# A mixer block with MLP on one core: first weight split over two DMA rings, and a new work order

## The chip, the core and the metric

The kernel runs on one core of one Trainium2 chip. The core has a matrix engine (PE, with weight loads shown as PEld), a vector engine (DVE), an activation engine (ACT), a general engine (POOL) and a sync engine (SP). Transfers between device memory and on-chip memory are issued by SP or by ACT; each of the two has a DMA queue ("ring") of its own. The metric is the device time of one execution, in microseconds (us): the median over several runs.

## The reference

`x` is 2048 tokens of 512 features, in bf16. The computation:

```python
h  = gelu(layernorm(x) @ w1)                       # w1: 512 x 512
# four quarters of h's features are shifted along the tokens by +1, -1, +2, -2
hs = concat(shift(h0, 1), shift(h1, -1), shift(h2, 2), shift(h3, -2)) @ w2   # w2: 512 x 512
x1 = x + hs
out = x1 + gelu(layernorm(x1) @ w3) @ w4           # w3: 512 x 1792, w4: 1792 x 512
```

The layer norms have no weights. The statistics are over the 512 features of a token.

## The kernel before

**Tiles.** The tokens form 16 tiles of 128 (t = 0 to 15). A tile passes through nine stages:

- Its load `dma_x` brings it into `x_sb`.
- Layer norm 1 (`ln`, lines 384 to 465). The statistics come from DVE (`bn_stats`, L416, and `bn_aggr`, L418) or from ACT (two activations with an accumulator, L395 and L400, and then small DVE operations, L408 and L412). POOL raises the variance to the power -1/2 (L423), and DVE, ACT or POOL normalizes (L445, L454, L457).
- A transpose puts features on the partitions, in `xnT`. It is done either by PE with an identity matrix (`pe_transpose`, L490, followed by a copy out of PSUM on DVE or ACT, L498), or by a DMA transpose issued on SP (L463).
- `up1` (`mm_up`, L626) multiplies by `w1`, and ACT applies gelu (L641) into `hT`.
- `mix` (`mm_mix`, L666) multiplies shifted slices of `hT` by `w2`; DVE adds `x` (L673 or L677) and makes `x1`. `mix` of tile t needs `hT` of tiles t-1, t and t+1.
- Layer norm 2 and its transpose work in the same way. Its numbers q run from 16 to 31: q = 16 + t.
- `up2` (L626) multiplies by `w3`, and ACT applies gelu (L641) into `h2T`.
- `down` (`mm_down`, L695) multiplies by `w4`, and DVE adds `x1` (L703).
- A DMA stores the tile.

Neighbouring tiles are grouped for `up1` and `up2` (`GROUPS`), in ones, twos and fours. In the written order `up1:6` means group 6 of layer 1. PSUM holds three double banks (`y_ps`) for transposes and `up`, and two banks (`o_ps`) for `mix` and `down`. So a `mix` waits until DVE has added up the `mix` or `down` two before it.

**The first tile** is special. It is centred only (L431), in two halves, and transposed in two halves (`sa:0`, `sb:0`). It is multiplied by `w1` in two halves, `ra:0` and `rb:0` (L528). The first half, two matmuls, reads the first half of `w1`; the second half reads the other. The scale goes into the gelu (L569), and `th:0` (L594) transposes the result.

**The order of PE** is written out in `SCRIPT`, from left to right. It begins with matmuls on zeros (`warm:9`, L720), which keep PE occupied until the first tile is ready; `ty:n` is a PE transpose of layer-norm output n, in a double bank. Output numbers that are not in `SCRIPT` as `sa` or `ty` are transposed by DMA.

**The order of the other engines** is not written out. `Program.order` gives each operation a due time, worked back from the PE order; `Program.place` then plays the program forward with its own estimates of durations and landings, and lets each engine take the most urgent operation that is ready. Engines run their lists in order, and wait with semaphores. `BIAS` adds to the due time of single operations. `NORM`, `EVAC`, `STAT_ACT`, `NMR` and `HEV` say which engine does which small operation, by q.

**The order of the loads** is `LOADS`, from left to right for each issuing engine. `@act` puts a load on ACT's ring; all others are on SP's. A suffix `a` or `b` means the first or second half of a weight's rows, and `x4-5` is one transfer of two tiles. An entry `tpN` fixes the place of a DMA transpose among the loads; if N is transposed by PE, the entry has no effect. Loads are issued ahead of all else on their engine (`op.first`). SP's list is in order: a DMA transpose that waits for its tile holds up every load behind it.

```python
LOADS = """
x1 x2 tp2 x0@act w1a w1b x3 x4-5 tp5 w2a w2b x6-7 w3 tp17 w4a x8-10 w4b tp6 x11-12 tp1 tp16 x13-15
"""
```

In this list `tp6` is the only `tp` entry that has an effect: the others are PE transposes.

Of the kernel before, what the change touches and what calls it, by code (L numbers as in the profile page):

```python
# [14 lines left out]
class Op:  # L15


    def __init__(self, name, eng, fn, reads, writes, dur, queue):
        self.name, self.eng, self.fn = name, eng, fn
        self.reads, self.writes = list(reads), list(writes)  # L20
        self.dur, self.queue = dur, queue
        self.idx = 0
        self.prio = 1e9
        self.first = None

class Program:
# [2 lines left out]

    HOP = {"pe": 200.0, "dve": 155.0, "act": 220.0, "pool": 120.0, "sp": 70.0}  # L30
    LOOK = {"dve": 300.0, "act": 300.0}
    DUE = 164483.0
    BEGIN = {"sp": 30.0, "act": 150.0, "pe": 400.0, "dve": 150.0, "pool": 450.0}
    ENTRY = 1900.0
    COLD, RESTART = 4300.0, 800.0
    LAG = {"load": 750, "tp": 700}

    def __init__(self):
        self.ops = []
# [12 lines left out]
    def order(self):  # L52
# [58 lines left out]
        assert seen == len(self.ops), "cycle"  # L111
        if self.DUE:

# [37 lines left out]
    def place(self, succs, order_only):  # L151

        npend = [len(d) for d in self.preds]
        ready = [0.0] * len(self.ops)
        cands = {e: [] for e in ENGINES}
        for op in self.ops:
            if npend[op.idx] == 0:
                cands[op.eng].append(op)
        free = dict(self.BEGIN)
        rings = {"sp": [], "act": []}  # L160
        fed = {}
        clock = moved = last = self.total = 0.0
        out = []

        def finish(limit):
            nonlocal clock
            while True:
                heads = {e: r[0] for e, r in rings.items() if r}
                if not heads:
                    return None  # L170
                live = [e for e in heads if heads[e][0] <= clock]
                later = min([h[0] for h in heads.values() if h[0] > clock], default=1e18)
                if not live:
                    if later > limit:
                        return None
                    clock = later
                    continue
                first = min(live, key=lambda e: heads[e][1])
                step = heads[first][1] * len(live)
                ends = clock + step <= min(later, limit)  # L180
                if not ends:
                    step = min(later, limit) - clock
                for e in live:
                    heads[e][1] -= step / len(live)
                clock += step
                if ends:
                    return rings[first].pop(0)[2]
                if clock >= limit:
                    return None

        def release(op, o, at):
            npend[o.idx] -= 1
            if at is not None:
                ready[o.idx] = max(ready[o.idx], at)
            if npend[o.idx] == 0:
                cands[o.eng].append(o)

        def land(op):
            nonlocal moved, last
            if op.queue == "tp":  # L200
                at = max(clock + 500.0, op.start + 2450.0, last + 600.0) + self.LAG["tp"]
            elif op.name.startswith("out"):
                at = clock + 300.0
                self.total = max(self.total, at)
            else:
                moved += op.dur
                at = clock + 600.0 + min(600.0, 0.3 * moved) + (600.0 if op.dur > 1400.0 else 0.0)
                at += self.LAG["load"] if moved > 1200.0 else 50.0
            if op.queue != "tp":
                last = max(last, at)  # L210
            op.landed = at
            for j in succs[op.idx]:
                if (op.idx, j) not in order_only:
                    release(op, self.ops[j], at + 30.0)

        while len(out) < len(self.ops):
            while True:
                best = None
                for e in ENGINES:
                    if cands[e]:  # L220
                        t = max(free[e], min(ready[o.idx] for o in cands[e]))
                        if best is None or t < best[0]:
                            best = (t, e)
                op = finish(best[0] if best else 1e17)
                if op is None:
                    break
                land(op)
            t, e = best
            look = self.LOOK.get(e, 1.0)
            op = min((o for o in cands[e] if ready[o.idx] <= t + look), key=lambda o: (o.prio, o.idx))  # L230
            cands[e].remove(op)
            start = max(free[e], ready[op.idx])
            op.start = start
            out.append(op)
            if op.queue:
# [6 lines left out]
                rings[e].append([start + (1400.0 if tp else 1000.0), work, op])  # L242
# [12 lines left out]
        while (op := finish(1e17)) is not None:  # L255
            land(op)
        self.seq = out
        return out

GROUPS = {1: (1, 1, 1, 1, 2, 1, 4, 2, 2, 1), 2: (2, 4, 4, 2, 4)}  # L260
NORM = {0: "act", 3: "act", 7: "pool", 8: "act", 9: "pool", 10: "pool", 11: "pool", 12: "pool", 14: "act", 15: "act", 16: "pool", 18: "act", 19: "act", 24: "pool", 25: "act", 26: "pool", 27: "pool", 29: "pool", 30: "pool", 31: "act"}
EVAC = {0: "both", 1: "both", 2: "both", 4: "both", 8: "both", 9: "dve", 10: "dve", 11: "dve", 12: "dve", 13: "dve", 14: "dve", 16: "dve", 17: "dve", 19: "both", 20: "both", 21: "both", 22: "both", 23: "both", 24: "dve", 25: "both", 27: "both", 29: "both", 30: "both", 31: "both"}
STAT_ACT = (0, 7, 9, 12, 13, 15, 18, 21, 25, 29, 30)
TAIL = (256, 160, 96)
NMR = {0: "pool", 1: "pool", 3: "pool", 5: "pool", 6: "pool", 7: "pool", 8: "pool", 9: "pool", 11: "pool", 13: "pool", 14: "pool", 15: "pool", 16: "pool", 17: "pool", 18: "pool", 20: "pool", 21: "pool", 22: "pool", 26: "pool", 27: "pool", 28: "pool", 29: "pool", 31: "pool"}
# [12 lines left out]
down:12-15  # L278
"""

def bass_standalone__mixer_s_mlp__prompt_kernel(nc, x, w1, w2, w3, w4, out):
# [14 lines left out]
    with ExitStack() as es:  # L296
        sb = lambda name, shape, dt: es.enter_context(nc.sbuf_tensor(name, shape, dt))
# [22 lines left out]
        warm = sb("warm", [P, 1], F32)  # L320
# [410 lines left out]
        for step in SCRIPT.split():  # L731
            kind, n = step.split(":")
# [139 lines left out]
```

## Time and profile before

| what | value |
|---|---|
| median of 4 runs | 135.58 us (135.18 to 135.88) |
| the profiled execution: its time | 135.58 us |
| the profiled execution: its span, first to last instruction | 134.3 us |
| PE busy, share of span | 131.1 us, 98% |
| DVE busy | 50.6 us, 38% |
| ACT busy | 58.6 us, 44% |
| POOL busy | 29.9 us, 22% |
| bytes moved by DMA | 12.19 MB |

The span leaves out 1.28 us of the execution's time. The profile page gives the busy time of each engine, the chain of work that ended last (followed back from the last instruction), and groups of instructions by code line with their count, busy time and mean duration. Other answers of the trace give the instructions in order of time, and the busy time and DMA rate in a stretch of the span. A row of the time-ordered list has the start, the length, the engine, the line, the operation and its tiles, the count, and in brackets the idle time before it and what ended that.

### The profile page before, as it was taken

The page shows a single profiled execution, that of the slowest core. Times are in us where ns is not written, and L with a number is a line of the kernel's source. Part 1 is how long each engine was busy: PE and PEld are TensorE (multiplying, and loading weights), DVE is VectorE, ACT ScalarE, POOL GpSimd, SP SyncE. Part 2 cuts the span into 40 slices and gives each one's busy share as a digit, 9 for nine tenths or more (in the row PEclk, how much of TensorE's full clock was granted, in tenths as well). Part 3 has the DMA queues.
Part 4 walks back from the last instruction along what each step waited for, and adds up shares of the span by engine and source line. Part 5 has one row for each costly group of instructions (what it writes and reads, how often), then busy time and mean ns, then how long its engine had stood idle before and what let it go on. Part 6 is the DMA issues. An engine that isn't in the chain of part 4 may idle for free.

```text
span 134.3 us, 2001 instructions
## 1 busy us (share of the span) xinstructions
PE 131.1 (98%) x776; PEld 71.7 (53%) x789; DVE 50.6 (38%) x134; ACT 58.6 (44%) x92; POOL 29.9 (22%) x68
## 2 busy tenths in 40 slices
PE   8999999999999999999999999999999999999994
PEld 3387687544666444478444444444444444444464
DVE  2799995765188930070061004232222200012223
ACT  6788359998535275547315554000000155520000
POOL 2444469983003850005010002100000000000000
PEclk9999999999999999999999999999999999999999
DMA  5899998445542134100311000311111100001112
GB/s 156 286 388 397 353 298 244 78 95 102 103 94 81 38 77 83 39 0 9 74 39 39 0 0 0 77 41 44 39 39 63 54 0 0 0 5 39 39 39 78
DMA packets 21289, 12.19 MB, mean 91 GB/s; under 512 B 13856, under 2 KB 20768, under 8 KB 21280
## 3 DMA queue, kind: packets, MB, share of 16 engines
q1 hardware_dynamic: 20704, 11.80, 32.1%
q10 hardware_dynamic: 576, 0.26, 0.7%
q8 instruction: 6, 0.10, 0.3%
q14 instruction: 3, 0.02, 0.1%
HBM read 6.82 MB, written 2.10 MB: 66 GB/s over the span
## 4 chain that ended last, share of the span: by engine, by line
PE 94%; DMA 3%; issue 1%; SPq 1%; DVE 0%
PE y_ps L626 46%; PE o_ps L695 36%; PE o_ps L666 10%; DMA w_sb<-in_w_dram 3%; PE y_ps L490 1%; PE y_ps L528 1%; SPq L368 1%; DVE o_sb L703 0%; PE o_ps L594 0%; SPq L857 0%
## 5 line engine op out<-in xcount | busy, mean ns | idle before, releaser
L626 PE MATMUL y_ps<-xnT,w_sb 128*128 128x512 bf16 (+2 forms) x421 | 63.4, 308 | 0.2
L626 PEld LDWEIGHTS y_ps<-xnT,w_sb 128*128 128x128 bf16 x424 | 38.3, 98 | 24.8
L641 ACT ACTIVATE h2T<-y_ps 128x1024 bf16<-128x1024 f32 (+1 forms) x29 | 28.6, 994 | 48.8 <-PE y_ps L626 48.6
L695 PE MATMUL o_ps<-w_sb,h2T 128*128 128x512 bf16 (+3 forms) x247 | 48.6, 355 | 0.3
L695 PEld LDWEIGHTS o_ps<-w_sb,h2T 128*128 128x128 bf16 x252 | 23.5, 98 | 24.7
L703 DVE TENSOR_TENSOR o_sb<-o_ps,x_sb 128x512 bf16<-128x512 f32 (+3 forms) x18 | 11.4, 632 | 47.5 <-PE o_ps L695 47.5
L423 POOL TENSOR_TENSOR rstd<-mv,neghalf 128x1 f32<-128x1 f32 x21 | 11.5, 551 | 22.9 <-DVE mv L418 13.2
L666 PE MATMUL o_ps<-w_sb,hT 128*128 128x512 bf16 x59 | 14.9, 379 | 0.3
L416 DVE BATCH_NORM_STATS2 st<-x_sb 128x6 f32<-128x512 bf16 x21 | 14.0, 677 | 2.7 <-DMA x_sb<-in_x_dram 2.6
L423 POOL TENSOR_TENSOR rstd<-vpe,neghalf 128x1 f32<-128x1 f32 x11 | 6.0, 550 | 29.6 <-DVE vpe L412 29.5
L673 DVE SCALAR_TENSOR_TENSOR x_sb<-o_ps,x_sb 128x512 bf16<-128x512 f32 x5 | 3.4, 686 | 19.2 <-PE o_ps L666 19.2
L641 ACT ACTIVATE hT<-y_ps 128x512 bf16<-128x512 f32 (+1 forms) x10 | 8.1, 808 | 5.7 <-PE y_ps L626 5.6
L677 DVE TENSOR_TENSOR x_sb<-o_ps,x_sb 128x512 bf16<-128x512 f32 x11 | 7.6, 687 | 4.8 <-PE o_ps L666 4.7
L666 PEld LDWEIGHTS o_ps<-w_sb,hT 128*128 128x128 bf16 x64 | 6.0, 98 | 5.7
L457 POOL TENSOR_SCALAR xn_buf<-x_sb,rstd,nmr 128x512 bf16<-128x512 bf16 x11 | 8.4, 770 | 0.8 <-DVE nmr L450 0.4
L400 ACT ACTIVATE junk<-x_sb 128x512 bf16<-128x512 bf16 x11 | 6.9, 626 | 2.3 <-DVE x_sb L673 2.2
L454 ACT ACTIVATE xn_buf<-x_sb,nmr,rstd 128x512 bf16<-128x512 bf16 x8 | 6.3, 806 | 0.3 <-POOL nmr L450 0.2
L445 DVE TENSOR_SCALAR xn_buf<-x_sb,mv,rstd 128x512 bf16<-128x512 bf16 x12 | 5.3, 443 | 2.8 <-POOL rstd L423 2.5
L720 PE MATMUL o_ps<-zeros 128*128 128x512 bf16 x9 | 4.0, 631 | 0.4 <-DVE zeros L347 0.4
L395 ACT ACTIVATE junk<-x_sb 128x512 bf16<-128x512 bf16 x6 | 3.7, 624 | 0.7 <-DMA x_sb<-in_x_dram 0.7
L418 DVE BATCH_NORM_AGGREGATE mv<-st 128x2 f32<-128x9 f32 x21 | 3.8, 188 | 0.3
L450 POOL TENSOR_SCALAR nmr<-mv,rstd 128x1 f32<-128x1 f32 x13 | 3.4, 266 | 0.7
(34 smaller groups left out, 28.8 us busy)
## 6 DMA issues: line engine op xcount, KB each, us to landing
out_dram<-o_sb SPq DMA_DIRECT2D x15, 128.0 KB, 1.7
w_sb<-in_w_dram SPq DMA_DIRECT2D x1, 1792.0 KB, 9.6
w_sb<-in_w_dram SPq DMA_DIRECT2D x2, 896.0 KB, 11.5
w_sb<-in_w_dram SPq DMA_DIRECT2D x4, 256.0 KB, 4.9
x_sb<-in_x_dram SPq DMA_DIRECT2D x3, 256.0 KB, 4.8
x_sb<-in_x_dram SPq DMA_DIRECT2D x2, 384.0 KB, 8.5
x_sb<-in_x_dram SPq DMA_DIRECT2D x3, 128.0 KB, 2.6
xnT<-xn_buf SPq DMA_TRANSPOSE x24, 2.5
```

The lines of the kernel that those rows point to most:

```text
L400: (lambda d: (lambda e: e.activation(d, src, ACT_F.Square, accum_out=sums[:, q, 1:2])))(junk[:, b, :]),
L416: pg.add("dve", f"bnst{q}", lambda e: e.bn_stats(st9[:, q, 0:6], src), reads=rs, writes=[(("st", q), 0)], dur=605)
L423: lambda e: e.tensor_tensor(col(rstd), var, neghalf[:], ALU.pow),
L445: lambda e: e.tensor_scalar(dst, src, mv[:, q, 0:1], rstd[:, q : q + 1], ALU.subtract, ALU.mult),
L454: f = lambda e: e.activation(dst, src, ACT_F.Identity, bias=nmr[:, q : q + 1], scale=rstd[:, q : q + 1])
L457: f = lambda e: e.tensor_scalar(dst, src, rstd[:, q : q + 1], nmr[:, q : q + 1], ALU.mult, ALU.add)
L626: ins = e.matmul(y_ps[:, p, W * i : W * (i + 1)], wsb[:, dc, P * fc : P * (fc + 1)], src[:, dc, P * t0 : P * t0 + W], start=(dc == 0), sto ...
L641: (lambda d, s: (lambda e: e.activation(d, s, ACT_F.Gelu_apprx_tanh)))(dst, ysrc),
L666: ins = e.matmul(dst, hT[:, j, c0 : c0 + P], w2_sb[:, j, :], start=(j == 0), stop=(j == DC - 1))
L677: f = lambda e: e.tensor_tensor(x1_sb[:, t, :], dst, x_sb[:, t, :], ALU.add)
L695: ins = e.matmul(dst, h2T[:, fc, P * t : P * (t + 1)], w4_sb[:, fc, cs], start=(fc == 0), stop=(fc == FC - 1))
L703: (lambda d, c: (lambda e: e.tensor_tensor(o_sb[:, oi, c], d, x1_sb[:, t, c], ALU.add)))(dst, cs),
```

## The change

- **Loads.** `w1`'s first half goes on ACT's ring, behind `x0` and ahead of `x3`, which moves there too. SP's ring has `x1`, `x2`, `w1`'s second half, and then single tiles and halves in another order. `w4`'s second half stands ahead of `w3`, which is loaded in two halves. There are 19 loads on SP and 3 on ACT, where there were 15 and 1. Of the `tp` entries only `tp16` has an effect (the others are PE transposes).
- **PE's order.** 11 matmuls on zeros in place of 9. PE transposes are 0 to 7 and 17, where they were 0 to 5, 16 and 17; so outputs 6 and 7 leave the DMA transposes and output 16 joins them. The groups of layer 1 keep their counts (six ones, three twos, one four) but stand in another order; those of layer 2 too (two twos, three fours). `mix`, `up` and `down` are in another order.
- **The small operations** are dealt to the engines anew, by tables.
- **The planner** that orders DVE, ACT, POOL and SP has other constants: a limit on the descriptors outstanding on SP's ring, another estimate of landings, another `DUE`, and biases on single operations. None of these is executed on the chip; they alter the order of each engine's list.

```diff
-    DUE = 164483.0
+    DUE = 67895.5
...
-    LAG = {"load": 750, "tp": 700}
+    RING = 150.0
+    LAG = {"load": 750, "tp": 350}
...
             if op.queue == "tp":
-                at = max(clock + 500.0, op.start + 2450.0, last + 600.0) + self.LAG["tp"]
+                turned = max(clock + 500.0, op.start + 2450.0, last + 500.0, turned + 480.0)
+                at = turned + self.LAG["tp"]
...
-                at += self.LAG["load"] if moved > 1200.0 else 50.0
+                at += 50.0 if moved <= 1200.0 else self.LAG["load"] - 300.0 if moved <= 4000.0 else self.LAG["load"] if moved <= 11000.0 else self.LAG["load"] + 650.0
...
+            if e == "sp":
+                over = op.descs - self.RING + sum(h[2].descs * h[1] / h[3] for h in rings[e])
+                at = clock
+                for h in rings[e]:
+                    if over <= 0:
+                        break
+                    at = max(at, h[0])
+                    n = h[2].descs * h[1] / h[3]
+                    at += h[1] * min(1.0, over / n)
+                    over -= n
+                    if over <= 0:
+                        start = max(start, at)
...
-GROUPS = {1: (1, 1, 1, 1, 2, 1, 4, 2, 2, 1), 2: (2, 4, 4, 2, 4)}
-NORM = {0: "act", 3: "act", 7: "pool", 8: "act", 9: "pool", 10: "pool", 11: "pool", 12: "pool", 14: "act", 15: "act", 16: "pool", 18: "act", 19: "act", 24: "pool", 25: "act", 26: "pool", 27: "pool", 29: "pool", 30: "pool", 31: "act"}
-EVAC = {0: "both", 1: "both", 2: "both", 4: "both", 8: "both", 9: "dve", 10: "dve", 11: "dve", 12: "dve", 13: "dve", 14: "dve", 16: "dve", 17: "dve", 19: "both", 20: "both", 21: "both", 22: "both", 23: "both", 24: "dve", 25: "both", 27: "both", 29: "both", 30: "both", 31: "both"}
-STAT_ACT = (0, 7, 9, 12, 13, 15, 18, 21, 25, 29, 30)
+GROUPS = {1: (1, 1, 1, 1, 1, 1, 2, 2, 4, 2), 2: (2, 4, 2, 4, 4)}
+NORM = {0: "act", 4: "act", 7: "pool", 9: "act", 11: "act", 13: "pool", 15: "act", 18: "pool", 19: "pool", 20: "pool", 21: "pool", 22: "pool", 24: "pool", 25: "pool", 27: "pool", 28: "act", 29: "act", 30: "act"}
+EVAC = {0: "dve", 2: "dve", 3: "dve", 5: "both", 7: "dve", 8: "both", 9: "both", 10: "dve", 11: "dve", 12: "both", 13: "both", 16: "both", 18: "both", 20: "dve", 21: "dve", 22: "both", 25: "dve", 26: "both", 27: "both", 28: "both", 31: "dve"}
+STAT_ACT = (0, 5, 6, 9, 11, 14, 15, 18, 22, 23, 25, 27, 28, 30, 31)
...
-HEV = {0: "dve", 4: "dve"}
-BIAS = {}
+HEV = {0: "dve", 1: "dve", 3: "dve", 5: "dve", 6: "dve"}
+BIAS = {"mean6": -214.811, "msq0": -704.156, "msq1": -1177, "msq3": -700, "msq8": 436, "nmr3": 872, "nmr5": -1644.96, "norm13": 252.578, "norm2": 835.299, "sum15": 16, "tp23": 764, "tp5": 433, "vpe11": -1349, "vpe2": 59, "x1_12": -296.043, "x1_2": 193, "x1_3": -58}
 LOADS = """
-x1 x2 tp2 x0@act w1a w1b x3 x4-5 tp5 w2a w2b x6-7 w3 tp17 w4a x8-10 w4b tp6 x11-12 tp1 tp16 x13-15
+x0@act tp0 x1 x2 w1b x6 x4 w2b tp6 w2a x5 tp2 x7 w4b tp2 x8 w3a w3b x9 x13 tp16 x11-12 w4a w1a@act tp7
+x14-15 x10 tp2 x3@act
 """
 SCRIPT = """
-warm:9 sa:0 sb:0 ty:1 ra:0 rb:0 ty:2 up1:1 th:0 up1:2 mix:0 ty:3 ty:5 mix:1 ty:4 up1:3-4 ty:16 mix:2 ty:17
-mix:3 up2:0 mix:4 up1:5 down:1 down:0 mix:5 up1:6-7 mix:8 mix:6 up1:9 mix:9-10 up1:8 mix:7 mix:11 up2:1
-mix:13 mix:15 up2:3 down:5 mix:12 up2:2 mix:14 down:2 down:4 down:3 down:6-8 down:11 down:9 up2:4 down:10
-down:12-15
+warm:11 sa:0 sb:0 ty:1 ra:0 rb:0 ty:2 up1:1 th:0 up1:2 ty:3 mix:0 up1:3 mix:1 ty:4 ty:6 mix:2 ty:7 up1:4
+ty:5 up1:6 up1:5 mix:3 ty:17 mix:5-6 up2:0 mix:4 up1:7 down:1 mix:7 up1:8 mix:8 down:0 mix:12 up1:9 mix:9
+mix:11 up2:1 mix:14 mix:10 up2:2 mix:13 down:2 mix:15 up2:3 down:5-6 down:4 down:3 up2:4 down:10 down:9
+down:8 down:13 down:7 down:14 down:11-12 down:15
 """
...
                 for op in load(item):
                     op.first = i - 100
+                    op.descs = 8.0 * len(op.writes)
                     queues[op.eng].append(op.name)
```

`NMR`, the table of the engines for the small product of mean and scale (L450), changes too and is left out here: 14 outputs are on POOL where 23 were, but only those count whose normalization is not on DVE.

More of the change, by code (lines that the diff above doesn't have):

```diff
@@ L22, in __init__ @@
         self.idx = 0
+        self.descs = 8.0
         self.prio = 1e9
@@ L161, in place @@
         fed = {}
-        clock = moved = last = self.total = 0.0
+        clock = moved = last = turned = self.total = 0.0
         out = []
@@ L198, in land @@
         def land(op):
-            nonlocal moved, last
+            nonlocal moved, last, turned
             if op.queue == "tp":
-                at = max(clock + 500.0, op.start + 2450.0, last + 600.0) + self.LAG["tp"]
+                turned = max(clock + 500.0, op.start + 2450.0, last + 500.0, turned + 480.0)
+                at = turned + self.LAG["tp"]
             elif op.name.startswith("out"):
@@ L241, in place @@
                 fed[e] = load
-                rings[e].append([start + (1400.0 if tp else 1000.0), work, op])
+                rings[e].append([start + (1400.0 if tp else 1000.0), work, op, work])
                 for j in succs[op.idx]:
@@ L258, in place @@
         return out
[L260 to L263 removed]
+GROUPS = {1: (1, 1, 1, 1, 1, 1, 2, 2, 4, 2), 2: (2, 4, 2, 4, 4)}
+NORM = {0: "act", 4: "act", 7: "pool", 9: "act", 11: "act", 13: "pool", 15: "act", 18: "pool", 19: "pool", 20: "pool", 21: "pool", 22: "pool", 24: "pool", 25: "pool", 27: "pool", 28: "act", 29: "act", 30: "act"}
+EVAC = {0: "dve", 2: "dve", 3: "dve", 5: "both", 7: "dve", 8: "both", 9: "both", 10: "dve", 11: "dve", 12: "both", 13: "both", 16: "both", 18: "both", 20: "dve", 21: "dve", 22: "both", 25: "dve", 26: "both", 27: "both", 28: "both", 31: "dve"}
+STAT_ACT = (0, 5, 6, 9, 11, 14, 15, 18, 22, 23, 25, 27, 28, 30, 31)
 TAIL = (256, 160, 96)
[L265 removed]
+NMR = {2: "pool", 3: "pool", 4: "pool", 6: "pool", 10: "pool", 12: "pool", 13: "pool", 16: "pool", 19: "pool", 21: "pool", 24: "pool", 25: "pool", 26: "pool", 31: "pool"}
 NAT = (0,)
```

## The prediction

> **What bounds the kernel now.** I read the page first: shares of busy time, and the chain that ended last.
>
> ```profile
> PE 131.1 (98%) x776; PEld 71.7 (53%) x789; DVE 50.6 (38%) x134; ACT 58.6 (44%) x92; POOL 29.9 (22%) x68
> PE 94%; DMA 3%; issue 1%; SPq 1%; DVE 0%
> ```
>
> PE is the bound, and the only other piece of weight is 3% of DMA. The chain in order of time tells where that lies:
>
> ```profile
> 0.99 4.54 DMA w_sb<-in_w_dram
> 5.53 0.05 issue
> 5.58 1.30 PE y_ps L528 x4
> 6.87 0.22 PE y_ps L490 x4
> 7.10 0.89 PE y_ps L626 x16
> ...
> 10.00 0.45 PE y_ps L490 x8
> ...
> 128.98 3.48 PE o_ps L695 x43
> 132.46 0.02 issue
> 132.49 0.26 DVE o_sb L703
> ```
>
> From 5.58 to 132.46 the chain is PE alone, with pieces of 0.05 "issue" between. So nothing behind the first tile's multiplication by `w1` (L528) can be gained by order: PE has 126.9 us to do from there, and the new order has the same matmuls. What can be gained lies ahead of 6.87. What can be lost is any wait that the new order puts on PE later, where there is none now.
>
> Next, PE's start: the weight loads in order of time.
>
> ```profile
> 2.97 0.15 PEld L720 LDWEIGHTS o_ps<-zeros 128*128 128x128 bf16 x1 [0.28 <-issue]
> 3.40 0.15 PEld L720 LDWEIGHTS o_ps<-zeros 128*128 128x128 bf16 x1 [0.28 <-issue]
> 4.20 0.90 PEld L490 LDWEIGHTS y_ps<-ident,xn_buf 128*128 128x128 bf16 x8 [0.65 <-POOL rstd L423]
> 5.57 0.13 PEld L528 LDWEIGHTS y_ps<-w_sb,xnT 128*128 128x128 bf16 x2 [0.48 <-DMA w_sb<-in_w_dram]
> 6.26 0.11 PEld L528 LDWEIGHTS y_ps<-w_sb,xnT 128*128 128x128 bf16 x2 [0.56 <-DMA w_sb<-in_w_dram]
> ```
>
> Both halves of `w1` are late: PE waits for the first until 5.57 and for the second until 6.26. The warm-up matmuls come every 0.43 us up to the last pair, and the eight transposes of 4.20 take 0.90; later, eight take 0.45 (the row at 10.00). So PE ran at half its clock until after 5.1, although the page's PEclk row shows 9 throughout; the trace's clock record has the full grant from 5.87 on.
>
> Last, the DMA rate in stretches (the last number of each row, GB/s).
>
> ```profile
> 1.50:2.25 0.75, 0.75 (x3) 0.28 (x2) 0.00 (x0) 0.61 (x2) 0.19 (x2) 1.00 0.97 332
> 2.50:3.25 0.75, 0.75 (x3) 0.30 (x2) 0.71 (x2) 0.42 (x1) 0.00 (x0) 1.00 0.60 154
> 3.25:4.00 0.75, 0.75 (x3) 0.15 (x1) 0.74 (x2) 0.72 (x4) 0.49 (x1) 1.00 0.51 142
> 4.75:6.00 1.25, 1.04 (x8) 0.48 (x6) 0.89 (x4) 1.22 (x4) 0.51 (x1) 1.00 1.03 353
> ```
>
> While `x0` ran on ACT's ring beside `x1` and `x2` on SP's, 332 GB/s flowed; then `w1` alone on SP's ring got 142 to 154; from 4.75 the single ring carried 353.
>
> **The change, part by part.**
>
> *w1 over both rings.* The Trainium skill ("DMA: Bandwidth & Descriptors", Issuing engines are not separate DMA queues) says that both rings end on the same 16 engines, and that spreading saves issue time only. By it `w1` still lands as a whole near 6.2, and PE's waits stay. The rows speak against it for this one stretch: two rings carried 332 where one carried 150. At 332, `w1`'s 524 KB, beginning near 2.3, are through at 3.9; with the 0.9 us that I allow from last byte to landing, both halves are there near 4.8, and near 5.4 if the gain is half of that. I take 5.1. The two waits are worth 0.42 (PE is free from 5.16) and about 0.3: at most 0.7 us together, if PE and its input are ready by then.
>
> *Eleven warm-ups for nine.* PE goes through its list in order. Nine end at 0.43 + 9 x 0.427 = 4.27, just as the first tile is ready (4.20). Eleven end at 5.13 while the clock is at half. Then come `sa`, `sb` and `ty:1`, eight transposes at 0.107, to 5.98. Both halves of tile 0 are now copied by DVE: `sa` is in at 5.34, about 0.3 of pipeline (PE to the copy at 4.98 in this trace), a copy of 0.28 and a hop of 0.1 give 6.0; `sb`'s copy follows by 6.3. So `ra` starts at 6.0 and `rb` at 6.43, ending at 6.86, where they end at 6.71 now: **+0.15**. `w1`'s earlier landing is then worth nothing, since PE comes later than it. The Trainium skill ("TensorE: Matmul & The Clock Gate", Part 1) says that the clock opens at the end of a free-running activity window of about 3.4 us, at a time that varies, however many matmuls that is. Under it the opening may fall between about 3.9 and 7.2. If it falls at 4.3, eleven end at 4.7, the transposes go at double rate, and `ra` can start at 5.4: `rb` ends at 6.28, or **-0.43**. If it falls after 6, both kernels slow down, and the change loses about 0.2. The one row that I have shows 5.87, so I take +0.15, and keep -0.43 and +0.25 for the range.
>
> *ACT's two more DMA issues* (0.47 + 0.38, by SP's rows for such loads) stand before the activation table load (0.62 to 1.90) and the statistics of tile 0 (2.83). These start about 0.15 later, which the warm-ups hide; with nine they would have delayed PE by as much.
>
> *One more PE transpose* (0, 1 to 7 and 17 against 0, 1 to 5, 16 and 17): four matmuls at 0.056, **+0.22** on PE, with nothing to hide it. The DMA transposes fall from 24 to 23; SP is not on the chain.
>
> *Layer-1 and layer-2 groups*: the same counts of each width, so the same matmuls: 0.
>
> *The loads.* Bytes ahead of each need, at before's landings: `w2` has the same 1,792 KB up to and with it, landed 8.75 then; `mix:0` comes at 6.86 + 0.22 + 0.89 + 0.22 + 0.89 + 0.22 = 9.3. Cover 0.5. `x7` and `x5` land by 9.5, as `x6-7` did, and are needed transposed at 13.2 and 14.3. With `w4`'s half and `x8` ahead, `w3` ends behind 4,864 KB, not 3,840; it landed at 14.1, so at 360 GB/s it lands near 17.0. `up2:0` follows `rb` by 13.13 us of PE work (eight transposes with `th`, six `up1` to layer-1 output of 0.89 or 1.75, six `mix` of 0.86), at 20.0. Cover 3.0. The small loads cost SP four more issues of 0.45; it has the time, because it waits for its ring or for tiles from 5.65 on.
>
> *tp16* is a new wait. Output 16 was a PE transpose and is now a DMA transpose at SP, with four loads (`x11-12`, `w4a`, `x14-15`, `x10`) queued behind it; `up2:0` waits for it. `mix:0` ends at 10.2; its sum, statistics, power and normalization took 3.95 us in this trace (10.00 to the end of POOL's normalization at 13.95), so it issues near 14.1. To landing a transpose takes
>
> ```profile
> xnT<-xn_buf SPq DMA_TRANSPOSE x24, 2.5
> xnT<-xn_buf SPq DMA_TRANSPOSE x1, 5.7
> ```
>
> 2.5 as a median, and 5.7 behind loads (the one issued at 15.59): 16.6 to 19.8, against 20.0. I take it as hidden, by 0.2 at the worst.
>
> *The dealing of small operations.* DVE normalizes 9 outputs of layer 1, not 6 (3 x 0.41), makes two more small products (0.4) and saves one statistics pair (0.5): about +1.1 us on an engine that is busy 14.4 of 16 us from 4 to 20. It still fits, with no slack to speak of. On the chain: 0, or up to 1 us if a late sum holds a `mix` bank or output 16.
>
> **Sum.** +0.15 + 0.22 = +0.37 on the profile's own 135.58 (134.3 of span and 1.28 around it), which is also the median of the runs: 135.95. In some executions the clock opens earlier, so I put the median at **135.9**.
>
> **The rivals.**
>
> *The start gains* (0.23): the clock opens by about 4.5, `w1` is there by 5.4. -0.43 + 0.22: 135.4. For it: warm-ups at full clock would be short. Against it: the trace's 5.87.
>
> *Slower* (0.26): `tp16` is late. DVE's fuller list puts the sum of tile 0 or output 16's statistics behind others by 1 us, and the transpose queues behind `w3`. Issued at 15.1, landing at 20.8, it stops PE at `up2:0` for 0.8: 136.7. It decides from an issue at 14.3 on if the landing is the 5.7 kind, and from 17.5 on if it is the 2.5 kind. For it: all waits of PE are covered by tenths now. Against it: only about 1 MB stands before the transpose in the ring by then.
>
> *The rings bring nothing* (0.06): `w1` lands at 6.2 or later because the rings share engines; PE waits for it at `rb`, and +0.22 to +0.5 remain: 136.0.
>
> **How the numbers follow.** The likeliest case, at 0.45, has 135.9 and a range of its own of 135.5 to 136.2. A measurement of this kernel can tell about 0.3%, or 0.41 us, so the marks are 135.17 and 135.99. Slower: a third of the likeliest case, all of `tp16`, half of the rings: 0.44. Faster: a quarter of the start's case, and a little of the likeliest: 0.07. Same: 0.49. The range reaches from the start's case to just beyond the late transpose: 135.3 to 136.9.
>
> **What would show it.** Warm-up weight loads still 0.43 apart and `sa`'s transposes at about 5.1; L528's loads waiting for the DVE copies, not for `w1`; `w1`'s loads landing near 5.1; 36 transposes' matmuls in the L490 group, not 32; no wait of PE between 7 and 132; the first DMA transpose issued near 14.1. I am wrong if PE waits anywhere behind the first tile, or if the chain begins with `w1` again.

## The result, and the profile after

The kernel after takes **136.07 us** (median of 38 runs, 135.29 to 136.52) against 135.58 us for the kernel before in the same session (135.14 to 136.08). The ratio (of the means) is 1.0028, with a 95% interval of 1.0020 to 1.0037: a loss of 0.28%, clear of the noise. The forecast was 135.9, in a range of 135.3 to 136.9. By the ratio the loss is inside the 0.3% that the prediction took as the least that can be told; by the medians it is 0.49 us, and 136.07 is just above its mark of 135.99.

The profiled execution of after took 135.82 us with a span of 134.3, where before's took 135.58, with a span of 134.3 too. It is one of the quicker executions: of the 39 times (38 and the profiled one) 14 lie from 135.29 to 135.91, and a dense group at 136.01 to 136.16 holds the median. The one profile thus doesn't show the usual course. Line numbers are 16 higher than before: 736 warm-ups, 506 PE transposes, 544 the first tile, 642 `up`, 682 `mix`, 711 `down`, 479 DMA transposes.

Shares of busy time, and engines on the chain that ended last, after:

```profile
PE 131.0 (98%) x782; PEld 72.0 (54%) x795; DVE 49.9 (37%) x147; ACT 61.0 (45%) x100; POOL 27.5 (21%) x60
PE 92%; DMA 4%; DVE 1%; issue 1%; SPq 1%; POOL 0%; DVEq 0%
```

PE is still the bound. Three counts are worth a look, since they return below: DVE has 147 instructions where it had 134, ACT 100 where it had 92, and POOL 60 where it had 68. The chain in order of time, after (start, length, what):

```profile
0.99 5.13 DMA w_sb<-in_w_dram
6.12 0.04 issue
6.17 0.60 PE y_ps L544 x2
6.77 0.24 PE y_ps L506 x4
7.03 0.42 DVE xnT L514
...
9.24 0.09 issue
9.32 0.81 PE o_ps L682 x3
...
20.00 6.11 PE y_ps L642 x56
```

It begins with `w1` again, which the prediction had named as a sign of being wrong. The piece at 9.32 is `mix:0`, the only wait of PE left behind the first tile. It counts 3 matmuls of 4: one record is missing, and its 0.22 us are part of the gap; about 0.05 is real. The weight loads at PE's start, after (start, length, in brackets the idle time and what ended it):

```profile
2.97 0.15 PEld L736 LDWEIGHTS o_ps<-zeros 128*128 128x128 bf16 x1 [0.28 <-issue]
3.40 0.15 PEld L736 LDWEIGHTS o_ps<-zeros 128*128 128x128 bf16 x1 [0.27 <-issue]
3.82 0.39 PEld L736 LDWEIGHTS o_ps<-zeros 128*128 128x128 bf16 x2 [0.28 <-issue]
4.38 0.68 PEld L506 LDWEIGHTS y_ps<-ident,xn_buf 128*128 128x128 bf16 x8 [0.17 <-issue]
5.27 0.13 PEld L544 LDWEIGHTS y_ps<-w_sb,xnT 128*128 128x128 bf16 x2 [0.21 <-issue]
6.16 0.11 PEld L544 LDWEIGHTS y_ps<-w_sb,xnT 128*128 128x128 bf16 x2 [0.77 <-DMA w_sb<-in_w_dram]
```

The warm-ups are 0.43 apart up to 3.82, and then two fall within 0.39: in this execution the clock opened between 3.82 and 4.12, not at 5.87. The eleven warm-ups ended early, `ra` started at 5.30 with its half of `w1` there (landed 4.35), and `rb` waited for the other half until 6.16. The DMA rate in the prediction's stretches, after (last number, GB/s):

```profile
1.50:2.25 0.75, 0.75 (x3) 0.29 (x2) 0.00 (x0) 0.63 (x1) 0.19 (x2) 1.00 0.96 302
2.50:3.25 0.75, 0.75 (x3) 0.30 (x2) 0.72 (x2) 0.74 (x3) 0.00 (x0) 1.00 0.94 318
3.25:4.00 0.75, 0.75 (x3) 0.30 (x2) 0.74 (x2) 0.72 (x3) 0.52 (x1) 1.00 1.02 277
```

The stretches in which `w1` alone had got 154 and 142 now carry 318 and 277, twice as much in this pair of profiles (the experiments below show how far that holds). Still `w1`'s second half landed at 6.12, before's second half having let PE go at 6.26.

The further waits that the prediction priced. The PE transposes' weight loads, and `tp16`, SP's only DMA transpose between 13 and 19 us, with its time from issue to landing (the three numbers are minimum, median and maximum of that one transpose):

```profile
L506 PEld LDWEIGHTS y_ps<-ident,xn_buf x36: 96/98/99, 4.4 to 18.0; 128*128 128x128 bf16 x36
14.46 1.26 SPq L479 DMA_TRANSPOSE xnT<-xn_buf  x1
DMA to landing us min/median/max: 4.2/4.2/4.2
```

36 transposing matmuls as forecast (nine transposes of four), at 0.098 of weight load like all others; `tp16` landed at 18.6, for an `up2:0` that began at 20.00 in the chain above.

**What the time is made of.** For each run I take the core's span (first to last instruction) from the device time, and call the rest the time outside the span. It is nearly constant in a kernel (1.26 to 1.39 in the single runs of before; the 1.28 given ahead of the prediction is one run, from a rounded span). Means, in us; those of before are from the three sessions of the experiments below, since the spans of the single runs are recorded there (in after's own session its mean time was 135.60):

| | device | span | outside |
|---|---|---|---|
| before | 135.55 | 134.23 | 1.32 |
| after | 135.97 | 134.44 | 1.53 |

So of the 0.42 us between these means, 0.21 lie within the span and **0.21 outside it**, where the prediction's sum had assumed no change.

### The profile page after: what moved, and what is told of

It is laid out like the page before. It is cut to its first block, busy times and chain, and to the rows that moved or that the text cites. A ratio compares the mean times of both kernels' runs of the same rounds, so it can differ in the third digit from the quotient of the medians.

```text
span 134.3 us, 2031 instructions
## 1 busy us (share of the span) xinstructions
PE 131.0 (98%) x782; PEld 72.0 (54%) x795; DVE 49.9 (37%) x147; ACT 61.0 (45%) x100; POOL 27.5 (21%) x60
## 4 chain that ended last, share of the span: by engine, by line
PE 92%; DMA 4%; DVE 1%; issue 1%; SPq 1%; POOL 0%; DVEq 0%
PE y_ps L642 44%; PE o_ps L711 36%; PE o_ps L682 10%; DMA w_sb<-in_w_dram 4%; PE y_ps L506 1%; SPq L384 1%; PE y_ps L544 0%; POOL rstd L439 0%; DVE xnT L514 0%; DVE xn_buf L461 0%; DVE hT L620 0%; DVE o_sb L719 0%; DVE mv L434 0%; DVE mv L424 0%; DVEq L838 0%
## 5 line engine op out<-in xcount | busy, mean ns | idle before, releaser
L439 POOL TENSOR_TENSOR rstd<-mv,neghalf 128x1 f32<-128x1 f32 x17 | 9.3, 552 | 27.5 <-DVE mv L421 13.5
L416 ACT ACTIVATE junk<-x_sb 128x512 bf16<-128x512 bf16 x15 | 9.4, 624 | 8.0 <-DVE x_sb L689 7.8
L432 DVE BATCH_NORM_STATS2 st<-x_sb 128x6 f32<-128x512 bf16 x17 | 11.6, 681 | 2.3 <-DMA x_sb<-in_x_dram 2.1
L439 POOL TENSOR_TENSOR rstd<-vpe,neghalf 128x1 f32<-128x1 f32 x15 | 8.3, 557 | 14.2 <-DVE vpe L428 14.1
L689 DVE SCALAR_TENSOR_TENSOR x_sb<-o_ps,x_sb 128x512 bf16<-128x512 f32 x8 | 5.5, 685 | 11.9 <-PE o_ps L682 11.9
L473 POOL TENSOR_SCALAR xn_buf<-x_sb,rstd,nmr 128x512 bf16<-128x512 bf16 x10 | 7.7, 776 | 1.1 <-DVE vpe L428 0.4
L461 DVE TENSOR_SCALAR xn_buf<-x_sb,mv,rstd 128x512 bf16<-128x512 bf16 x14 | 6.2, 444 | 2.9 <-POOL rstd L439 2.8
L470 ACT ACTIVATE xn_buf<-x_sb,nmr,rstd 128x512 bf16<-128x512 bf16 x7 | 5.6, 807 | 3.1 <-DVE nmr L466 3.1
L693 DVE TENSOR_TENSOR x_sb<-o_ps,x_sb 128x512 bf16<-128x512 f32 x8 | 5.4, 677 | 4.2 <-PE o_ps L682 4.0
L411 ACT ACTIVATE junk<-x_sb 128x512 bf16<-128x512 bf16 x7 | 4.4, 623 | 0.0
L466 DVE TENSOR_SCALAR nmr<-mv,rstd 128x1 f32<-128x1 f32 x11 | 2.3, 209 | 4.0 <-POOL rstd L439 4.0
```

The costliest lines, as they stand in the source:

```text
L416: (lambda d: (lambda e: e.activation(d, src, ACT_F.Square, accum_out=sums[:, q, 1:2])))(junk[:, b, :]),
L432: pg.add("dve", f"bnst{q}", lambda e: e.bn_stats(st9[:, q, 0:6], src), reads=rs, writes=[(("st", q), 0)], dur=605)
L439: lambda e: e.tensor_tensor(col(rstd), var, neghalf[:], ALU.pow),
L461: lambda e: e.tensor_scalar(dst, src, mv[:, q, 0:1], rstd[:, q : q + 1], ALU.subtract, ALU.mult),
L470: f = lambda e: e.activation(dst, src, ACT_F.Identity, bias=nmr[:, q : q + 1], scale=rstd[:, q : q + 1])
L473: f = lambda e: e.tensor_scalar(dst, src, rstd[:, q : q + 1], nmr[:, q : q + 1], ALU.mult, ALU.add)
```

## The experiments

All ran beside the kernel before, whose median was 135.49 to 135.56 in these sessions; its span's mean was 134.21 to 134.27 and its outside time 1.32. "Outside" below is the time outside the span. In each, the list of the order is left alone unless said.

### Two more warm-ups, alone

```diff
-                for _ in range(n):
+                for _ in range(11):
```

> The kernel before, with 11 warm-up matmuls issued where it has 9; every engine's order as before. Theory A (the warm-ups are a cost of the change): in executions whose clock opens after about 5.1 us the first tile's product ends about 0.15 later (6.86 for 6.71), in the others nothing changes because w1's landing at 6.2 covers it; so +0.1 to +0.2, about 135.7. Rival B (w1's landing covers the warm-ups always): 135.58. The time outside the span stays 1.3 in both.

Measured: 135.94 us, ratio 1.0024 [1.0012, 1.0035]; span's mean 134.51, outside 1.32. The loss of 0.39 (0.30 by the means) is larger than expected. Its profile shows where it lies: PE's weight loads and then ACT's gelu of the first tile, in that kernel:

```profile
6.05 0.56 PEld L528 LDWEIGHTS y_ps<-w_sb,xnT 128*128 128x128 bf16 x4 [0.24 <-issue]
6.73 0.42 PEld L490 LDWEIGHTS y_ps<-ident,xn_buf 128*128 128x128 bf16 x4
7.11 0.94 PEld L626 LDWEIGHTS y_ps<-xnT,w_sb 128*128 128x128 bf16 x16
8.22 0.23 PEld L594 LDWEIGHTS o_ps<-ident,hn 128*128 128x128 bf16 x4 [0.17 <-ACT hn L569]
```

```profile
7.48 0.69 ACT L569 ACTIVATE hn<-y_ps,rstd 128x512 bf16<-128x512 f32 x1 [0.66 <-POOL rstd L423]
```

The first tile's multiplication is no longer held by `w1`; it runs through without a gap. Then `th:0` waits for the gelu `hn`, which waited for POOL's `rstd`: 0.16 there and 0.13 at the next group, measured as gaps between matmuls. In before's profile this wait is covered: `rstd` was ready at 6.60, and `hn` began at 6.98, held by `rb`, which had waited for `w1`. The kernel after, and the three variants of it below, which keep its dealing of the small operations, show no such wait in their profiles.

### The kernel after with nine warm-ups

```diff
-                for _ in range(n):
+                for _ in range(9):
```

> The kernel after, with 9 warm-up matmuls issued where it has 11; every engine's order as in the kernel after. Theory A: -0.1 to -0.25 against 136.07, so about 135.87, and fewer executions at 136.07. Rival B (the loss is elsewhere): 136.07. The time outside the span stays 1.53 in both.

Measured: 135.78 us, ratio to before 1.0017 [1.0001, 1.0034]; span's mean 134.21, outside 1.54. Against after's 136.07 that is 0.29 less (0.23 by the span's means). So the two warm-ups cost 0.23 in the kernel after and 0.30 in the kernel before, by the means of the span; each figure is good to about 0.15 to 0.2. Without them the span is that of the kernel before, although one more PE transpose is in it (0.24, next section): something else in the change gains about as much, see the sum below. The 0.2 that the kernel is still slower lie outside the span.

### One more PE transpose

```diff
-                    for c in range(c0, c1):
+                    for c in [*range(c0, c1)] * (2 if q == 17 else 1):
```

> The kernel before, with the four PE transposes of layer-norm output 17 issued twice, into the same place. Theory A (each PE transpose more is on the path): +0.22, 135.80. Rival (PE has slack there): 135.58, at most 0.09 less than theory A by the one wait of 0.09 that the trace of before has at 11.2.

Measured: 135.80 us, 1.0019 [1.0005, 1.0033], the span's mean 134.46: +0.24 to +0.25 for four matmuls. PE's work behind the start has no cover, as the prediction took it.

### The time outside the span: semaphores and loads

The change has 19 loads on SP where there were 15. Two runs ask whether the count of semaphores (shared here: 39 for DMA, not 58) or the count of loads (three loads of several tiles, cut into single tiles) makes the 0.21.

```diff
...
-            op.stream = ("dma", ndma)
-            sems[op.stream] = es.enter_context(nc.semaphore(f"sem_dma{ndma}"))
-            ndma += 1
+            op.stream = ("dma", op.share or ndma)
+            if op.stream not in sems:
+                sems[op.stream] = es.enter_context(nc.semaphore(f"sem_dma{ndma}"))
+                ndma += 1
...
```

> The kernel before, same instructions in the same order, with 39 DMA semaphores in place of 58: the stores of one output slot share one, and the DMA transposes out of one slot share one. Theory C (the time outside the span, 1.31 before and 1.53 after, grows with the number of DMA semaphores, 58 and 63, by 0.044 each): 19 x 0.044 = 0.84 less, 134.75, all of it outside the span (0.47). Rival D (it goes with the number of instructions or of transfers, which stay): 135.58, 1.31 outside the span.

Measured: 135.45 us, 1.0002 [0.9988, 1.0015], outside 1.33. Semaphores are not it.

```diff
+        for name, t0, n in (("dma_x4", 4, 2), ("dma_x6", 6, 2), ("dma_x8", 8, 3)):
...
+            op.fn = lambda e, t=t0: e.dma_start(x_sb[:, t, :], xt[:, t, :])
...
```

> The kernel before, with its loads of tiles 4-5, 6-7 and 8-10 issued as seven loads of one tile each, at the same place of SP's list: 19 loads on SP's ring, as in the kernel after. Theory A (SP has time for more issues): 135.58, within 0.1. Rival (issues of 0.45 delay w2 or w3): +0.2 or more. The time outside the span is 1.53 if it goes with the number of loads on SP's ring (G), 1.32 otherwise.

Measured: 135.53 us, 1.0000 [0.9982, 1.0018], outside 1.32. Nor is it the number of loads.

### w1's first half on ACT's ring, alone, and with x3

```diff
...
+        for name, eng, by, past in [('dma_w1a', 'act', 'dma_x0', 1)]:
+            op = at[name]
+            op.eng, op.queue, op.start = eng, eng, at[by].start
+            seq.remove(op)
+            seq.insert(seq.index(at[by]) + past, op)
```

> The kernel before, with w1's first half moved to ACT's ring behind x0, and nothing else changed: every other instruction in the same order on its engine. Theory A (the split alone is a gain, which the warm-ups of the change give away): both halves land earlier, PE's two waits for w1 shrink, -0.1 to -0.4, about 135.3. Rival, by the skill's rule that both rings end on the same engines: the second half still lands near 6.1, 135.5 to 135.6. If loads on ACT's ring make the time outside the span (E), it is 1.42 here; otherwise 1.32.

Measured: **135.14 us**, 0.9970 [0.9955, 0.9984], outside 1.33: faster than both kernels. The weight loads of its profiled execution (135.52 us, one of its longer ones: 19 of 22 are shorter), its chain's engines, and its DMA rate in two of the stretches:

```profile
5.22 0.14 PEld L528 LDWEIGHTS y_ps<-w_sb,xnT 128*128 128x128 bf16 x2 [0.16 <-DMA w_sb<-in_w_dram]
5.80 0.10 PEld L528 LDWEIGHTS y_ps<-w_sb,xnT 128*128 128x128 bf16 x1 [0.44 <-DMA w_sb<-in_w_dram]
6.06 0.15 PEld L528 LDWEIGHTS y_ps<-w_sb,xnT 128*128 128x128 bf16 x1 [0.15 <-issue]
```

```profile
PE 98%; DVE 0%; issue 0%; DVEq 0%
2.50:3.25 0.75, 0.75 (x3) 0.30 (x2) 0.72 (x3) 0.72 (x3) 0.00 (x0) 1.00 0.77 180
3.25:4.00 0.75, 0.75 (x3) 0.15 (x1) 0.64 (x2) 0.72 (x4) 0.56 (x1) 1.00 0.80 191
```

PE goes on at 5.22 and 5.80 where it had waited until 5.57 and 6.26, and DMA has left the chain. But this profile doesn't show how the gain comes about. The rate is 180 and 191, not doubled, and in another profile with `w1` on one ring (the run above with its loads cut into single tiles) PE goes on at 5.21 and 5.94, nearly as here. The landings vary from one execution to the next, so I take all profiles of this case together (GB/s, and us from the span's start):

| first loads | profiles | 2.50 to 3.25 | 3.25 to 4.00 | `w1`'s second half landed |
|---|---|---|---|---|
| `w1` on SP's ring, `x0` alone on ACT's | 7 | 83 to 205 | 85 to 254 | 5.60 to 6.44 |
| `w1`'s first half on ACT's ring behind `x0` | 2 | 180, 318 | 191, 280 | 5.76, 5.20 |
| the same with `x3` behind it | 4 | 318 to 359 | 277 to 329 | 5.50 to 6.72 |
| `w1` on SP's ring, `x0` and `x3` on ACT's | 1 | 249 | 216 | 6.04 |

The more there is on the second ring, the more flows in these stretches; but the second half of `w1` doesn't land earlier for it. The gain of the split alone is clear by its times. Whether it comes from the rate isn't shown: the move also takes one DMA issue off SP, so that `w1`'s second half is issued at 0.99 and not at 1.47, which is 0.48 by itself. No run separates the two.

The second run moves `x3` there too, behind `w1`'s half, as the change does:

```diff
-        for name, eng, by, past in [('dma_w1a', 'act', 'dma_x0', 1)]:
+        for name, eng, by, past in [('dma_w1a', 'act', 'dma_x0', 1), ('dma_x3', 'act', 'dma_w1a', 1)]:
```

> As the run before this, with x3 moved to ACT's ring too, behind w1's first half. Theory F (x3 on ACT's ring takes engine time from w1's second half): the second half lands 0.2 to 0.4 later than with w1 alone, and the gain is 0.1 to 0.2 smaller. Rival: the same time as with w1's half alone. If loads on ACT's ring make the time outside the span (E), it is 1.53 here, as in the kernel after; otherwise 1.32.

Measured: 135.52 us, 1.0003 [0.9985, 1.0021], outside 1.32. The gain is gone. Theory F's reason is not seen: in this run's profile `w1`'s second half landed at 5.50, earlier than the 5.76 of the run without `x3`. The profile has two other costs that the run without `x3` has not: the statistics of tile 0 begin at 3.03 on ACT instead of 2.63, behind a third DMA issue of 0.49, so that the transposes begin at 4.42 instead of 4.26; and the wait of `th:0` for `hn` (0.29 in all) appears. But this profiled execution was one of the quicker ones (135.28, of 135.14 to 136.52), and the one without `x3` one of the longer, so what makes the medians isn't shown.

### The kernel after with w1 on one ring

```diff
...
+        for name, eng, by, past in [('dma_w1a', 'sp', 'dma_w1b', 0)]:
...
```

> The kernel after, with w1's first half moved back to SP's ring, ahead of the second; x3 stays on ACT's ring, and every other instruction keeps its place. Theory A (11 warm-ups hide when w1 lands): 0 to +0.15 against 136.07. Rival (the split is worth its two waits): +0.3 or more. The time outside the span is 1.42 if it goes with loads on ACT's ring (E), 1.53 otherwise.

Measured: 136.05 us, 1.0032 [1.0018, 1.0046], outside 1.53; after had 136.07. In the kernel after, splitting `w1` is worth nothing, to within about 0.15. The profiled execution (136.09, where after's times lie densest) has the clock opening at 5.93. PE's matmuls at its start:

```profile
5.11 1.00 PE L506 MATMUL y_ps<-ident,xn_buf 128*128 128x128 bf16 x8
6.01 1.02 PE L544 MATMUL y_ps<-w_sb,xnT 128*128 128x512 bf16 x4
6.87 0.39 PE L506 MATMUL y_ps<-ident,xn_buf 128*128 128x128 bf16 x4
7.09 1.06 PE L642 MATMUL y_ps<-xnT,w_sb 128*128 128x128 bf16 x16
```

Transposes from 5.11, `ra` at 6.01, no wait for `w1` even on one ring, the next group at 6.87: the prediction's course for eleven warm-ups (5.13, 6.0, 6.86), almost to the hundredth. Other executions with eleven warm-ups differ. In after's own profile, and in that of the last run below (the kernel after with 9 more POOL instructions, 136.43 us), PE waits for `w1`'s second half although `w1` is split; in the latter its weight load is this (L546 there is L544 in after):

```profile
6.76 0.11 PEld L546 LDWEIGHTS y_ps<-w_sb,xnT 128*128 128x128 bf16 x2 [0.81 <-DMA w_sb<-in_w_dram]
```

### Split and eleven warm-ups together

The two edits above, of `w1`'s half alone and of the warm-ups alone, in the kernel before.

> The kernel before with w1's first half on ScalarE's ring (0.42 faster alone) and 11 warm-ups for 9 (0.39 slower alone), all else kept. Theory: both act on PE's start and don't add: the warm-ups end near 5 to 6 us, so the first tile's multiplication starts there whenever w1 lands, and the split's gain is gone: 135.9, as with 11 warm-ups alone. Rival: the two are independent and add: 135.5. Time outside the span 1.32 by both.

Measured: 135.60 us, 1.0005 [0.9989, 1.0022], outside 1.32, single times from 135.0 to 136.0. By the means it is 0.12 slower than before, give or take 0.19. My theory (warm-ups alone: +0.30) and the rival (the sum of both: -0.10) lie near the two ends of that, so this run doesn't decide between them. In the profiled execution the clock opened early (the eight transposes take 0.61, not 0.90), `ra` started at 5.70, held by a copy of ACT and not by `w1`. That fits a split which pays in executions whose clock opens early, and not in the others; the runs don't show the clock of each execution, so it is argued only. Of four pairs of medians, each as the distance to its session's kernel before, one gain is clear: without `x3` beside it the split gains 0.42 with nine warm-ups (from 0 to -0.42). With eleven it is 0.28 (from +0.39 to +0.11; 0.18 by the means, within the noise of 0.21). With `x3` there it is 0.04 (from 0 to -0.04), and 0.00 in the kernel after (from +0.49 to +0.49).

### The time outside the span: the engines' programs

What is left is the number of instructions, of one engine or of all. Each run adds small operations on a scratch buffer to one engine; none of them feeds anything.

```diff
...
-                       (lambda d, c: (lambda e: e.tensor_tensor(o_sb[:, oi, c], d, x1_sb[:, t, c], ALU.add)))(dst, cs),
+                       (lambda d, c, n: (lambda e: [*(e.memset(scr[:, k : k + 1], 0.0) for k in range(n)),
+                                                    e.tensor_tensor(o_sb[:, oi, c], d, x1_sb[:, t, c], ALU.add)][-1]))(
+                           dst, cs, 19 if (t, hh) == (2, 0) else 0),
```

> The kernel before with 19 more VectorE instructions, small memsets of a scratch buffer ahead of tile 2's last sum, where VectorE waits for PE; it computes the same. Theory H, the time outside the span goes with the length of VectorE's program (this edit brings it to that of the kernel after): outside the span 1.53 instead of 1.32, in all 135.8. Rivals I (ScalarE's program) and J (GpSimd's): outside 1.32, in all 135.55 to 135.65.

Measured: 135.81 us, 1.0019 [1.0005, 1.0034], and **outside 1.53**. The busy line of its profile:

```profile
PE 131.2 (98%) x789; PEld 71.4 (53%) x789; DVE 50.4 (38%) x153; ACT 58.3 (43%) x92; POOL 29.7 (22%) x68
```

153 instructions on DVE, everything else as in the kernel before. The other 0.1 of the difference lie in the span (mean 134.34 for 134.21), which is within the noise.

```diff
...
-                       (lambda d, s: (lambda e: e.activation(d, s, ACT_F.Gelu_apprx_tanh)))(dst, ysrc),
+                       (lambda d, s, n: (lambda e: [*(e.activation(scr[:, k : k + 1], eps_c[:], ACT_F.Gelu_apprx_tanh)
+                                                      for k in range(n)),
+                                                    e.activation(d, s, ACT_F.Gelu_apprx_tanh)][-1]))(
+                           dst, ysrc, 7 if (layer, g, f0) == (2, 1, 0) else 0),
```

> The kernel before with 7 more ScalarE instructions, activations of one element a partition ahead of one gelu of the second block; it computes the same. Theory I, the time outside the span goes with the length of ScalarE's program: outside the span 1.53, in all 135.8 or more. Rivals H and J: outside 1.32, in all 135.55 unless a gelu comes late for PE (at most 7 x 0.2 us).

Measured: 135.51 us, 1.0001 [0.9989, 1.0013], outside 1.32.

```diff
...
-            pg.add("pool", "pad1", lambda e: e.memset(hT[:, :, HTW - 2 : HTW], 0.0),
+            pg.add("pool", "pad1", lambda e: [*(e.memset(scr[:, k : k + 1], 0.0) for k in range(9)),
+                                              e.memset(hT[:, :, HTW - 2 : HTW], 0.0)][-1],
```

> The kernel after with 9 more GpSimd instructions, small memsets of a scratch buffer beside the padding's own; it computes the same. Theory J, the time outside the span grew because GpSimd's program became shorter: outside the span 1.32, in all 135.85. Rivals H and I: outside 1.53, in all 136.05 unless the memsets (9 x 0.1 us) delay a first statistic.

Measured: 136.14 us, 1.0038 [1.0024, 1.0052], outside 1.53. The instructions in the traces, beside the time outside (before's own profile lacks 13 matmul records; the run with the split alone has the same instructions and all records):

| kernel | DVE | all engines | outside |
|---|---|---|---|
| before | 134 | 2014 | 1.32 |
| before, 7 more on ACT | 134 | 2021 | 1.32 |
| before, `ty:17` issued twice | 134 | 2022 | 1.33 |
| before, 19 more on DVE | 153 | 2033 | 1.53 |
| after, nine warm-ups | 147 | 2040 | 1.54 |
| after, `w1` on one ring | 147 | 2044 | 1.53 |
| after, 9 more on POOL | 147 | 2053 | 1.53 |

So 19 more instructions on DVE are enough for the whole 0.21. That POOL's program became shorter is not the cause, and 7 more on ACT alone are not enough (after has 8 more). A cost in proportion to DVE's count would have been 0.31 for the 19 if it was 0.21 for 13, so it looks like a step. Two readings of the step fit every row: it lies between 134 and 147 instructions of DVE, or between 2022 and 2033 of all engines together. No run adds as many instructions to another engine, so that it is DVE's program, and not the number of all instructions, isn't shown. What happens in that time is open.

## Why the prediction held, point by point

**PE is the bound, and behind the start the matmuls are the same: held.** From 7 us on after's PE has one wait of 0.05. Strictly, this wait and the chain that begins with `w1` are the two signs of being wrong that the prediction had named; both came, and in after's profile they are worth 0.05 and 0.28.

**Eleven warm-ups, +0.15 with a clock opening at 5.87: held for that opening, mis-sized over the executions.** The course with the clock at 5.93 came out as worked out (6.01 and 6.87 for 6.0 and 6.86), and `up1:1` began there at 7.09, for 6.93 in before's trace: +0.16. Over all executions of the kernel after, the two warm-ups cost 0.23 in the span's mean, and 0.29 in the median. The opening does vary, as the Trainium skill has it ("TensorE: Matmul & The Clock Gate", Part 1), but more widely than the 500 ns either way that the page gives. It came at 4.77, 5.01, 5.57, 5.68, 5.75, 5.87, 5.93 and 6.36 in the profiles of this case that have a record of it. By the spacing of the matmuls it came between 3.82 and 4.12 in after's, between 3.40 and 3.71 in the run with 19 more on DVE, and before 3.35 in the run with fewer semaphores: earlier than the 3.9 that the prediction took as the earliest. A single trace gives one draw.

**One more PE transpose, +0.22: held** (0.24 to 0.25 measured).

**w1 over both rings: the landing failed, and the rate held only in part.** The prediction set one profile's rows (332 for 150 GB/s) against the rule of the Trainium skill ("DMA: Bandwidth & Descriptors", Issuing engines are not separate DMA queues) that spreading saves issue time only. With the split and `x3` all four profiles do carry 277 to 359 in these stretches; with the split alone one of two carries only 180 and 191. The gain of 0.42 from moving one load doesn't refute the rule, since the issue time saved is 0.48. "Both halves are there by 5.1" counted `w1`'s bytes as if the second rate was theirs alone. In after's profile the halves landed at 4.35 and 6.12, and in the four with `x3` the second half at 5.50 to 6.72; that `x3` and the next tiles take its share is likely, but theory F's run didn't show it. That the split is worth nothing in the kernel after held, but not for the stated reason alone (PE comes later than `w1`): in two of the three profiles with eleven warm-ups and the change's dealing PE did wait for the second half, 0.28 and 0.32 between its matmuls, and these are the two with `w1` split. With `x3` on the ring the split is worth nothing in the kernel before either.

**ACT's DMA issues, hidden behind the warm-ups: seen in profiles, its cost not isolated.** Tile 0's statistics begin on ACT at 3.02 in after's profile and at 2.83 in before's, for a forecast of 0.15 later. With nine warm-ups this was to delay PE: the first transposes begin at 4.42 in both such runs with `x3` on ACT's ring, for 4.25 in before's profile. The run with `x3` is slower than the one without by 0.38, which is the right sign, but no run takes the delay apart from the rest.

**The loads and tp16: held.** `tp16` issued at 14.46 (14.1), landed at 18.6 (16.6 to 19.8); `w3`'s second half landed at 17.37 (17.0); `up2:0` began at 20.00 (20.0). The slower rival asked for an issue after 14.3 with a landing of 5.7; it got the issue, but a landing of 4.2.

**The dealing of small operations, 0: this term failed, in both directions.** On the chain it was worth a little: before's wait of 0.09 at 11.24 is gone, and so is the wait of `th:0` for `hn`, which would have taken 0.29 of the start as soon as `w1` no longer held PE. Off the chain, **0.21 came up outside the span**, a place that the sum took as fixed. The new dealing has 13 more DVE instructions, and 19 more of them in the kernel before do the same; whether their number on DVE or the number of all instructions counts is open. The prediction asked only where DVE's time goes, and not what more instructions cost otherwise.

**The sum.** From before's profile to the one with the clock at 5.93 the last matmul moves from 132.24 to 132.54, +0.29: 0.16 for the warm-ups, 0.22 for the transpose, less the 0.09. With 0.21 outside it makes +0.50; 136.09 less 135.58 is 0.51. For this pair of profiles the forecast of +0.37 before the allowance for early clocks was thus 0.08 too high within the span and 0.21 too low outside. By the means of all runs the span grew by 0.21 only: 0.23 for the warm-ups and 0.24 for the transpose make 0.47, so the rest of the change gained about 0.26. The wait at 11.24 is 0.09 of that; the remainder isn't isolated, and with an uncertainty of some 0.2 it may be less. So 135.9 came near 136.07 partly by luck: the span grew less than forecast, and the time outside it grew where nothing was forecast.

## What to carry to other kernels

Take the time outside the span for each kernel before reading traces: here half of the difference lay in it, and no row of a trace shows it. Where PE waits on a start-up load, moving that one load to a second ring can pay, as the 0.42 here; but measure it by times, put nothing else behind it there without measuring, and don't take a higher rate for an earlier landing. Look, too, at what PE would wait for next, since the gap you close may cover it. When a single execution's start depends on when the clock opens, compare many times, and use the profiles only for the course of events.

## What the runs showed of the hardware that was not expected

- The time outside the span is 1.32 us with 134 DVE instructions (at most 2022 in all) and 1.53 us with 147 and with 153 (at least 2033 in all); 7 more on ACT, 9 more on POOL, 2 or 4 more matmuls with their weight loads on PE, 4 more loads on SP or 19 fewer DMA semaphores don't move it.
- One load of 256 KB moved to the second ring gained 0.42 us of 135.56; a second one of 128 KB behind it took that back. With both there, 277 to 359 GB/s flowed between 2.50 and 4.00 us, where 83 to 254 flowed without, and yet `w1`'s second half landed at 5.50 to 6.72 us, against 5.60 to 6.44.
- The clock opened before 3.35 us in one profile and at 6.36 in another, in kernels whose PE starts alike, at 0.43 to 0.45.
